# A projection slot between the value product and the next score pair, and lower halves 19 instead of 18 slots behind

## The chip, the cores and the metric

The kernel runs on one core of one Trainium2 chip. The metric is the device time of one execution in microseconds; the time of a kernel is the median of its runs.

## The reference

The kernel computes a gated mix of two branches over the same input `x` of 2048 tokens with 512 features, all in float32.

```python
def ref(x, wqkv, wo, w_gate, w_up, w_down, gate_w):
    g = sigmoid((x * gate_w).sum(-1, keepdims=True))
    # branch a: 32 heads of 16 features, each query sees the 256 keys up to itself
    q, k, v = split_heads(x @ wqkv)
    scores = where(mask, q @ k.T * 16 ** -0.5, -1e9)
    a = merge_heads(softmax(scores) @ v) @ wo
    # branch b: hidden width 1376
    b = (sigmoid(x @ w_gate) * (x @ w_up)) @ w_down
    return g * a + (1 - g) * b
```

## The kernel before

Products of float32 accuracy are made of three products of shorter operands: each operand is split into a high and a low part, and high times high, high times low and low times high are summed in PSUM. For the projections (queries and keys, called `pj`; gate and up, called `gu`) one output tile of 128 x 512 takes 12 such matmuls, 4 blocks of the contraction times 3.

The 32 heads are worked in 8 groups of 4, and the 2048 tokens in 16 blocks of 128. One step `u` of the main loop is one block of one group, so there are 128 steps and some more to drain. In a step the 4 heads `hh` are gone through one after the other. For each head one **turn** is put into TensorE's queue:

- `s_part` (line 296): scores with queries on partitions, into a PSUM tile `s`. VectorE takes the row maximum of it (line 302, tile `junk`, then `mx`).
- `st_part` (line 342): scores of block `u - 9` with keys on partitions, into a PSUM tile `st`, of another head. ScalarE takes the exponential of it into `pt` (line 347). The two score matmuls use 64 rows of the array each, one the upper and one the lower 64, so that they run side by side: a score pair.
- a stretch of **slots** of the projections. `turns()` is a generator. In slot number t it issues one matmul for the upper 64 rows of the contraction (matmul t of a long list in which each projection tile has 12), and one for the lower 64 rows, which stands `SHIFT` slots further back in the list. The two run side by side on the two halves of the array and both add into PSUM. So a projection tile (a **group**) occupies its PSUM buffer for 12 slots of its upper half and until `SHIFT` slots later its lower half is through too. A turn takes `GAP` = 3 slots; the fourth turn of an odd step takes none. Two steps so have 7 turns with 21 slots.

When the lower half of a group is through, `turns()` appends its evacuation to the list `evac`: ScalarE copies the PSUM tile to SBUF (`gu_post`, line 466, or `proj_raw`, line 240), and what follows from that copy (a DMA of it, the next weights' split by `gu_next`). `flush(evac)` is called after the score pair of each turn, so the copy stands in ScalarE's queue behind the exponential of that turn. The projections' PSUM pool `misc` has 3 buffers, so the first matmul of a group takes the buffer of the group three before it, and waits for that group's copy.

At the start of each even step, before the score pair of its first head, the **value products** `pv_part` of two earlier blocks are issued (line 378): matmuls with 32 columns of the array for each of 4 heads, which take all 128 rows.

Every 16th step and so on other work is spread in the same hand-made order: `split_wqk`, `split_gu` (the next weights' high and low parts), `max_split`, `o_take` (line 394, evacuation of `pv`), and DMAs on SyncE's queue, collected in `later` and issued at the head of a step. The order of the instructions on TensorE, ScalarE, VectorE and SyncE is the order written (the schedule is manual); the framework only adds the waits between engines.

After the main loop come the drain steps (`u` of 128 and more, no `s_part`), in which six slots stand after each second head, and then the down projection (`pd`) and the output projection (`pa`), which the change doesn't touch.

```python
for half, v in enumerate((t, t - SHIFT)):
    if 0 <= v < n_rest * k3:
        groups[v // k3][0](v % k3, half)
if t >= SHIFT and (t - SHIFT) % k3 == k3 - 1:
    _, after, post = groups[(t - SHIFT) // k3]
    evac.append(lambda after=after, post=post: (post(), after()))
```

Of the kernel before, what the change touches and what calls it, by code (L numbers as in the profile page):

```python
# [36 lines left out]
PVLAG = LAG + 2  # L37
# [1 line left out]
QB = 32  # L39
HOLD = 3  # L40
GAP = 3
SHIFT = 18
WD_LATE = {1: 8, 2: 9, 5: 10}
AHEAD = 5

# [2 lines left out]
def gated_mix_kernel(  # L48
# [48 lines left out]
    NU = NG * NB  # L97
# [15 lines left out]
    with ExitStack() as actx:  # L113
# [12 lines left out]
        def load_wqk(g):  # L126
            raw = cpool.tile([P, ND, P], F32, tag="wqraw", name=f"wqraw{g}", bufs=2)
            nc.sync.dma_start(raw, wqk[g])
            return raw
# [126 lines left out]
        def stack_build(t):  # L256
            sh, sl = (v.bitcast(F32) for v in stg.pop(t))
            rt = ring[t % RING].bitcast(F32)
            st = rt.rearrange("(a r) j f -> r a j f", r=4)
            dmas = [fill_rows(t % RING, 0, 0)]  # L260
            for low in range(2):
                for j in range(4):
                    for r in range(3):
                        if low == (r == (1 if j < 2 else 2)):
                            dmas.append((st[r + 1, :, j], (sl if low else sh)[32 * j:32 * j + 32]))
            return dmas
# [52 lines left out]
        def max_store(s):  # L319
            nt = nms.pop(s)  # L320
            dst = max_d[s].rearrange("h l b (a t) -> a (h l b) t", t=QB)
            for a in range(P // QB):
                nc.sync.dma_start(dst[a], nt[a * QB:(a + 1) * QB])
# [40 lines left out]
        evac = []  # L364
# [4 lines left out]
        def pv_part(u):  # L369
            g, j = divmod(u, NB)  # L370
            p = pts.pop(u)
            last = min(NB, j + 3)
            q = j
            while q < last:
                e = min(last, (q // 4 + 1) * 4)
                for hh in range(HG):
                    h = g * HG + hh
                    mm(  # L378
                        pv[32 * hh:32 * hh + 32, (q % 4) * P:(q % 4 + e - q) * P],
                        V[:, j, h * VW:h * VW + 32],  # L380
                        p[:, hh, (q - j) * P:(e - j) * P],
                        start=False, stop=True, skip_group_check=True,
                        tile_position=(0, 32 * hh),
                    )
                q = e
            if j % 2 == 1:
                extras.append(lambda: o_take(g * NC + j // 4, j // 2 % 2))

        def o_take(s, half):
            g, c = divmod(s, NC)  # L390
            if half == 0:
                obs[s] = cpool.tile([P, CH], F32, tag="ob", name=f"ob{s}", bufs=2)
            cols = slice(2 * P * half, 2 * P * half + 2 * P)
            nc.scalar.copy(obs[s][:, cols], pv[:, cols])
            nc.vector.memset(pv[:, cols], 0.0)
            if half == 0:
                return
            ob = obs.pop(s)
            for hh in range(HG):
                h = g * HG + hh  # L400
                later.append((oT_d[h * DH:(h + 1) * DH, c * CH:(c + 1) * CH], ob[32 * hh:32 * hh + DH]))
            later.append((sum_d[c, g * HG:(g + 1) * HG], ob.rearrange("(h r) f -> r h f", r=32)[DH]))
# [38 lines left out]
        def load_gu(f, w):  # L441
            raw_gu[f, w] = cpool.tile([P, D], F32, tag="draw", name=f"guraw{f}_{w}", bufs=2)
            src = wgu[f, w] if FCH[f] == P else wgu_tail[w, :, :, 0:width(f, w)]
            nc.sync.dma_start(gu_half(raw_gu[f, w], width(f, w)), src)
# [69 lines left out]
        def turns():  # L514
            k3 = 3 * ND
            groups = []
            for t in range(n_rest * k3 + SHIFT):
                if t and t % GAP == 0:
                    yield
                if t % k3 == 0 and len(groups) < n_rest:  # L520
                    groups.append((work or rest).pop(0))
                for half, v in enumerate((t, t - SHIFT)):
                    if 0 <= v < n_rest * k3:
                        groups[v // k3][0](v % k3, half)
                if t >= SHIFT and (t - SHIFT) % k3 == k3 - 1:
                    _, after, post = groups[(t - SHIFT) // k3]
                    evac.append(lambda after=after, post=post: (post(), after()))

        def flush(acts):
            while acts:  # L530
                acts.pop(0)()
# [24 lines left out]
        def flat(v, c):  # L556
            return v[c].rearrange("h (q t) -> (h q) t", t=P)
# [5 lines left out]
        def sums_invert(c):  # L563
            t = sm.pop(c)
            nc.vector.reciprocal(t, t)
            return flat(rec_d, c), t

        n_first = len(first) * 3 * ND + 2 * 3 * ND
        n_rest = len(rest) + NSTEP - 6 - HOLD
# [4 lines left out]
        WD = NU - 5  # L574
        done = 0
        slots = turns()
        sdma = []

        for u in range(N):
            if u == LAG:  # L580
                vctx.close()
                ppool = actx.enter_context(tc.tile_pool(name="ppool", bufs=1))
            if u == 4:
                load_gu(0, 0)
                load_gu(0, 1)
            if u % 8 == 1 and u > 8 and u // 8 + 1 < NP:
                sdma = stack_build(u // 8 + 1)
            if u % 16 == 8 and u // 16 + 2 < NG:
                raw_q = load_wqk(u // 16 + 2)
            if u % 4 == 0 and 0 < u <= NU:  # L590
                max_store(u // 4 - 1)
            run_dmas(later)
            later.clear()
            run_dmas(sdma[:SD])
            del sdma[:SD]
            if u % 4 == 1 and 1 < u <= NU + 1:
                max_load(u // 4 - 1)
            if WD <= u < WD + 16 and (u - WD) % 2 == 0:
                load_d((u - WD) // 2)
            s4 = {1: 4, 5: 5, 9: 6, U_LAST: NSTEP - 2, U_LAST + 1: NSTEP - 1}.get(u)  # L600
            if u % 4 == 3 and u > LAG and (u + 2) // 4 + 4 < NSTEP - 2:
                s4 = (u + 2) // 4 + 4
            if s4 is not None:
                if u < LAG:
                    (work if u == 1 else first).append((3 * ND, lambda k, s4=s4: proj_mm(s4, k), lambda s4=s4: proj_post(s4)))
                else:
                    work.append(proj_group(s4))
            for hh in range(HG):
                if hh == 0 and u % 2 == 0:
                    for w in (u - PVLAG - 1, u - PVLAG):  # L610
                        if 0 <= w < NU:
                            pv_part(w)
                if u < NU:
                    s_part(u, hh)
                if 0 <= u - LAG < NU:
                    st_part(u - LAG, hh ^ 1 if u < NU else hh)
                flush(evac)
                flush(behind)
                if u >= LAG and (hh < HG - 1 or u % 2 == 0 if u < NU else hh % 2 == 1):
                    next(slots, None)  # L620
                    if u >= NU:
                        next(slots, None)
            flush(extras)
            extras.extend(extras_next)
            extras_next.clear()
            if u < LAG - 1:
                done += run_first(n_first * (u + 1) // LAG - done)
            elif u < LAG:
                run_first(n_first - done - 3 * ND)
                split_gu(0, 0)  # L630
                split_gu(0, 1)
                flush(behind)
                run_first(3 * ND)
                done = 0
            if u % 4 == 3 and u < NU:
                max_split(u // 4)
            if u // 16 + 2 < NG:
                if u % 16 == 13:
                    split_wqk(u // 16 + 2, raw_q, 0)
                if u % 16 == 14:  # L640
                    split_wqk(u // 16 + 2, raw_q, 1)
            if 0 <= u - LAG < NU:
                mask_p(u - LAG)
            if WD + 2 <= u < WD + 10 and (u - WD) % 2 == 0:
                split_d((u - WD) // 2 - 1)
            if SUMS <= u and (u - SUMS) % 4 == 0:
                sums_load((u - SUMS) // 4)
            if SUMS + 2 <= u and (u - SUMS) % 4 == 2:
                later.append(sums_invert((u - SUMS) // 4))
            if u >= HLOAD and (u - HLOAD) % 2 == 0:  # L650
                h_load((u - HLOAD) // 2)
            if u >= N - 2:
                h_skew(u - N - 1)
# [162 lines left out]
```

## Time and profile before

| what | value |
|---|---|
| median of 3 runs | 772.11 us (771.64 to 774.44) |
| the profiled execution: time, span | 771.27 us, 769.6 us |
| TensorE (PE) busy | 754.3 us, 98% |
| VectorE (DVE) busy | 477.4 us, 62% |
| ScalarE (ACT) busy | 438.9 us, 57% |
| GpSimd (POOL) busy | 169.1 us, 22% |
| DMA | 103.57 MB, mean 135 GB/s |

PE stands for TensorE's matmuls and PEld for its weight loads. In a group's row of the profile stand its instructions' busy time, the mean duration of one in ns, and the time that the engine stood idle just before them with what ended it. Rows of the timeline begin with start and duration in us, and end with the idle time before in brackets.

### The profile page before, as it was taken

To read this page: it belongs to the slowest core of one execution; us is meant where nothing else is said; L and a number is where in the kernel's file an instruction comes from. 1 tells how busy PE (TensorE), PEld (TensorE's weight loads), DVE (VectorE), ACT (ScalarE), POOL (GpSimd) and SP (SyncE) were. 2 spreads that over 40 slices of the span, in tenths; PEclk is the share of its full clock that TensorE was granted. 3 is DMA by queue.
4 is the path that set the end of the run, shared out by engine and by line. 5 is a ranking of instruction groups with operands and counts; after the bars stand their busy time and mean duration, and the time that the engine had idled before them with its cause. 6 is when DMAs were issued, how large, how long until landed. Compare 5 with 4: busy or idle time off the path is not lost.

```text
span 769.6 us, 17398 instructions
## 1 busy us (share of the span) xinstructions
PE 754.3 (98%) x6180; PEld 575.0 (75%) x6180; DVE 477.4 (62%) x1459; ACT 438.9 (57%) x930; POOL 169.1 (22%) x256
## 2 busy tenths in 40 slices
PE   8999999999999999999999999999999999999998
PEld 6877777776867777777777777777775778888886
DVE  5356766666676666666666677567621694739371
ACT  5412666676666666666667666665765563625341
POOL 7000333232233232323323322332331000000000
PEclk9999999999999999999999999999999999999999
DMA  8340424425443353342543425443265786647351
GB/s 300 91 111 18 114 86 107 135 81 159 118 106 110 119 138 111 92 137 84 159 126 94 121 69 146 136 129 100 99 190 174 229 253 205 202 163 244 109 162 55
DMA packets 69958, 103.57 MB, mean 135 GB/s; under 512 B 19314, under 2 KB 29042, under 8 KB 69872
## 3 DMA queue, kind: packets, MB, share of 16 engines
q1 hardware_dynamic: 69872, 102.48, 45.3%
q8 instruction: 48, 0.79, 0.4%
q14 instruction: 38, 0.31, 0.1%
HBM read 45.26 MB, written 32.00 MB: 100 GB/s over the span
## 4 chain that ended last, share of the span: by engine, by line
PE 83%; DVE 5%; ACT 4%; DMA 3%; issue 2%; SPq 1%; POOLq 0%; ACTq 0%; DVEq 0%
PE gu L228 30%; PE pv L378 9%; PE pj L228 8%; PE s L296 8%; PE st L342 5%; PE pd L72 4%; PE pd L70 4%; PE pd L71 4%; PE vps L70 2%; PE vps L71 2%; PE vps L72 2%; PE pa L70 2%; PE pa L72 2%; PE pa L71 2%; DVE junk L302 1%
## 5 line engine op out<-in xcount | busy, mean ns | idle before, releaser
L347 ACT ACTIVATE pt<-st 128x384 f32<-128x384 f32 (+2 forms) x512 | 241.1, 474 | 182.8 <-PE st L342 79.1
L228 PE MATMUL gu<-xh,w 64*128 64x512 f32 (+2 forms) x1384 | 343.4, 392 | 0.0
L302 DVE CUSTOM_DVE_ANT_0 junk<-s,mask 128x384 f32<-128x384 f32 (+2 forms) x512 | 270.4, 528 | 114.7 <-PE st L342 42.3
L228 PE MATMUL gu<-xl,w 64*128 64x512 f32 (+2 forms) x692 | 226.3, 392 | 0.0
L228 PEld LDWEIGHTS gu<-xh,w 64*128 64x128 f32 (+3 forms) x1384 | 189.0, 183 | 20.6 <-issue 0.2
L296 PE MATMUL s<-ring 64*128 64x384 f32 (+2 forms) x536 | 169.8, 339 | 6.6 <-DVE mx L302 5.3
L342 PE MATMUL st<-ring 64*128 64x384 f32 (+2 forms) x536 | 173.1, 338 | 0.0
L352 POOL TENSOR_SCALAR_AFFINE_SELECT pt<-pt 128x512 f32<-128x512 f32 x128 | 82.3, 643 | 402.0 <-ACT pt L347 398.4
L296 PEld LDWEIGHTS s<-ring 64*128 64x128 f32 x536 | 94.2, 184 | 60.7 <-DVE mx L302 37.0
L228 PEld LDWEIGHTS gu<-xl,w 64*128 64x128 f32 (+2 forms) x692 | 107.0, 183 | 5.9
L342 PEld LDWEIGHTS st<-ring 64*128 64x128 f32 x536 | 96.1, 184 | 12.3 <-issue 1.4
L378 PE MATMUL pv<-pt,V 128*32 128x384 f32 (+2 forms) x1408 | 91.0, 388 | 1.7 <-POOL pt L352 1.7
L228 PE MATMUL pj<-xh,wqh 64*128 64x512 f32 (+1 forms) x232 | 91.0, 397 | 0.7 <-ACT xh L66 0.7
L228 PE MATMUL pj<-xl,wqh 64*128 64x512 f32 (+1 forms) x232 | 90.8, 396 | 0.4 <-DVE xl L67 0.4
L357 POOL TENSOR_SCALAR_AFFINE_SELECT pt<-pt 128x512 f32<-128x512 f32 x112 | 77.3, 690 | 0.0
L228 PE MATMUL pj<-xh,wql 64*128 64x512 f32 (+1 forms) x232 | 71.6, 395 | 0.0
L72 PE MATMUL pd<-ring,hb 128*128 128x512 f32 (+1 forms) x176 | 69.4, 394 | 0.3 <-DVE hb L67 0.3
L70 PE MATMUL pd<-ring,hb 128*128 128x512 f32 (+1 forms) x176 | 69.5, 395 | 0.0
L71 PE MATMUL pd<-ring,hb 128*128 128x512 f32 (+1 forms) x176 | 68.8, 391 | 0.4 <-DVE ring L67 0.4
L378 PEld LDWEIGHTS pv<-pt,V 128*32 128x32 f32 x1408 | 37.3, 109 | 36.9 <-issue 28.8
L66 ACT CAST hb<-V 128x512 fp32r<-128x512 f32 (+1 forms) x44 | 27.3, 621 | 54.5 <-DVE V L552 53.8
L466 ACT COPY sp<-gu 128x512 f32<-128x512 f32 (+2 forms) x88 | 51.0, 581 | 1.2 <-issue 1.2
(74 smaller groups left out, 900.0 us busy)
## 6 DMA issues: line engine op xcount, KB each, us to landing
gu_scratch<-sp SPq DMA_DIRECT2D x80, 256.0 KB
V<-gu_scratch SPq DMA_DIRECT2D x80, 256.0 KB
ring<-sh SPq DMA_DIRECT2D x128, 128.0 KB
ring<-sl SPq DMA_DIRECT2D x64, 128.0 KB
guraw<-in_wgu_dram SPq DMA_DIRECT2D x20, 256.0 KB
V<-in_xT_dram SPq DMA_DIRECT2D x16, 256.0 KB
oT_scratch<-ob SPq DMA_DIRECT2D x128, 32.0 KB
xl<-oT_scratch SPq DMA_DIRECT2D x16, 256.0 KB
```

The source lines that it names most:

```text
L70: mm(ps, lh, rh, start=first, stop=False)
L71: mm(ps, lh, rl, start=False, stop=False)
L72: mm(ps, ll, rh, start=False, stop=last)
L228: mm(pt[0:fw], (wl if w == 2 else wh)[r, d], (xl if w == 1 else xh)[r, d, c * CH:(c + 1) * CH], start=k == 0 and half != 1, stop=k == 3 * ...
L296: mm(pt[:, (k - k0) * P:(e - k0) * P], lhsT, blk(g, k, hh, 1, e - k), start=k == k0, stop=e == i + 1, skip_group_check=True,)
L302: nc.vector.tensor_tensor_reduce(junk[:, 0:n], pt[:, 0:n], mask[:, 3 * P - n:], scale=1.0, scalar=NEG, op0=ALU.add, op1=ALU.max, accum_out ...
L342: mm(pt[:, (q - j) * P:(e - j) * P], lhsT, blk(g, q, hh, 0, e - q), start=q == j, stop=e == last, skip_group_check=True,)
L347: nc.scalar.activation(pts[u][:, hh, 0:n], pt[:, 0:n], AF.Exp, scale=SCALE)
L352: nc.gpsimd.affine_select(p[:, :, 0:P], p[:, :, 0:P], pattern=[[0, HG], [1, P]], compare_op=ALU.is_ge, fill=0.0, base=0, channel_multiplie ...
L357: nc.gpsimd.affine_select(p[:, :, 2 * P:], p[:, :, 2 * P:], pattern=[[0, HG], [-1, P]], compare_op=ALU.is_gt, fill=0.0, base=0, channel_mu ...
L378: mm(pv[32 * hh:32 * hh + 32, (q % 4) * P:(q % 4 + e - q) * P], V[:, j, h * VW:h * VW + 32], p[:, hh, (q - j) * P:(e - j) * P], start=Fals ...
L466: nc.scalar.copy(t[0:width(f, w)], gp.pop((f, c, w))[0:width(f, w)])
```

## The change

`SHIFT` is 19 instead of 18. `turns()` yields after each slot instead of after each third, and `run_slots(n)` runs n of them. At the head of each even step, after the value products and before the score pair of its first head, `evac` is flushed and one slot is run. The first turn of that step then runs two slots instead of three, so that two steps have 21 slots as before (in the drain steps the turn after the second head gives the slot). Number and kinds of all instructions are the same as before on every engine.

```diff
-SHIFT = 18
+SHIFT = 19
...
             for t in range(n_rest * k3 + SHIFT):
-                if t and t % GAP == 0:
-                    yield
                 if t % k3 == 0 and len(groups) < n_rest:
...
                     evac.append(lambda after=after, post=post: (post(), after()))
+                yield
...
+        def run_slots(n):
+            for _ in range(n):
+                next(slots, None)
...
                         if 0 <= w < NU:
                             pv_part(w)
+                head = u > PVLAG and hh == 0 and u % 2 == 0
+                if head:
+                    flush(evac)
+                    run_slots(1)
                 if u < NU:
                     s_part(u, hh)
...
                 if u >= LAG and (hh < HG - 1 or u % 2 == 0 if u < NU else hh % 2 == 1):
-                    next(slots, None)
-                    if u >= NU:
-                        next(slots, None)
+                    run_slots((GAP if u < NU else 2 * GAP) - (u > PVLAG and u % 2 == 0 and hh == (0 if u < NU else 1)))
```

## The prediction, made before the changed kernel ran

> **What bounds the kernel now.** I read the page first: the span, the busy shares, the granted clock and the chain that ended last, then the costliest groups.
>
> ```profile
> span 769.6 us, 17398 instructions
> ...
> PE 754.3 (98%) x6180; PEld 575.0 (75%) x6180; DVE 477.4 (62%) x1459; ACT 438.9 (57%) x930; POOL 169.1 (22%) x256
> ...
> PEclk9999999999999999999999999999999999999999
> ...
> PE 83%; DVE 5%; ACT 4%; DMA 3%; issue 2%; SPq 1%; POOLq 0%; ACTq 0%; DVEq 0%
> ...
> L228 PE MATMUL gu<-xh,w 64*128 64x512 f32 (+2 forms) x1384 | 343.4, 392 | 0.0
> L296 PE MATMUL s<-ring 64*128 64x384 f32 (+2 forms) x536 | 169.8, 339 | 6.6 <-DVE mx L302 5.3
> ```
>
> TensorE is the bound: 98% busy at full clock, 83% of the chain. It stands idle 15.3 us in the whole span, and the only idle time of weight inside the attention loop is before the score matmuls (6.6 us, mostly for VectorE's row maximum). Before the projection matmuls it is 0.0: no slot waits today. Since TensorE executes in order and has no slack, whatever makes one matmul wait is added to the time in full, and whatever takes idle time away can bring no more than these few us. The next view, the waits of TensorE alone, says the same:
>
> ```profile
> PE s L296 <- DVE mx L302: 5.3, 12, 0.8
> PE pv L378 <- POOL pt L352: 1.7, 1, 1.7
> ```
>
> There is no row in which a projection matmul in the loop waits for ScalarE, although every group takes a PSUM buffer that ScalarE must have copied out. How near that copy comes to being late is read in the timeline of one turn, here one in which a group (pj) has just ended:
>
> ```profile
> 306.83 0.33 PE L342 MATMUL st<-ring 64*128 64x384 f32 x1
> 306.84 0.34 PE L296 MATMUL s<-ring 64*128 64x384 f32 x1
> 307.00 0.40 PE L228 MATMUL gu<-xh,w 64*128 64x512 f32 x2
> 307.24 0.40 PE L228 MATMUL gu<-xl,w 64*128 64x512 f32 x2
> 307.24 0.49 ACT L347 ACTIVATE pt<-st 128x384 f32<-128x384 f32 x1 [0.39 <-PE s L296]
> 307.47 0.40 PE L228 MATMUL gu<-xh,w 64*128 64x512 f32 x2
> 307.63 0.58 ACT L240 COPY pr<-pj 128x512 f32<-128x512 f32 x1
> 307.70 0.33 PE L296 MATMUL s<-ring 64*128 64x384 f32 x1
> 307.71 0.33 PE L342 MATMUL st<-ring 64*128 64x384 f32 x1
> 307.87 0.39 PE L228 MATMUL gu<-xh,w 64*128 64x512 f32 x1
> 308.57 0.34 PE L342 MATMUL st<-ring 64*128 64x384 f32 x1
> 308.74 0.39 PE L228 MATMUL pj<-xh,wqh 64*128 64x512 f32 x1
> ```
>
> A turn is 0.87 us: the score pair 0.17 (306.83 to 307.00), then three slots of 0.23. The group's last matmul was the slot before 306.83. The exponential of this turn begins at 307.24, the copy behind it at 307.63, and the copy ends at 308.21 (307.63 + 0.58). The third group after it takes the freed buffer at 308.74, two turns after the pair at 306.83. So the copy is 0.53 us ahead of its user, which is less than one turn.
>
> **The change, part by part.**
>
> *The lag of 19.* A group begins at slot 12n and ends at slot 12n + 29 before, 12n + 30 after; its buffer is wanted at slot 12n + 36 in both. Turns end at slots divisible by 3. So before, the last matmul closes a turn, and the copy is queued with the next turn's exponential. After, the last matmul opens a turn (or is the head slot); two more slots follow it, and the copy is queued only behind the exponential of the turn after that. In ScalarE's order the copy therefore stands one exponential, one turn of 0.87 us, further back, while its user stays where it was. In the rows above it is as if the user came at 307.87, with the copy still ending at 308.21: 0.34 us late.
>
> What a late release costs beyond its lateness is read where VectorE releases a score matmul late:
>
> ```profile
> 216.64 0.49 ACT L347 ACTIVATE pt<-st 128x384 f32<-128x384 f32 x1 [0.26 <-PE s L296]
> 217.87 0.08 DVE L302 DVE_READ_ACCUMULATOR2_ANT mx<- 128x1 f32 x1
> 218.00 0.18 PEld L296 LDWEIGHTS s<-ring 64*128 64x128 f32 x1 [1.17 <-DVE mx L302]
> 218.01 0.45 PE L296 MATMUL s<-ring 64*128 64x384 f32 x1 [0.74 <-DVE mx L302]
> 218.01 0.18 PEld L342 LDWEIGHTS st<-ring 64*128 64x128 f32 x1
> 218.29 0.39 PE L228 MATMUL gu<-xh,w 64*128 64x512 f32 x2
> ```
>
> VectorE is done at 217.95 (217.87 + 0.08) and the weight load starts at 218.00: 0.05 us. It is the weight load that waits, so it is not hidden behind an earlier matmul: from the score pair to the next slot it is 0.28 us here, against 0.17 in the turn above, 0.11 more. One late group thus costs 0.34 + 0.05 + 0.11 = 0.50 us. Behind the waiting load stand, in TensorE's one queue, the lower half of the same slot, the other slots of the turn and the next score pair, and so the next row maximum and the next exponential: nothing on TensorE gets past it.
>
> *How many groups are late.* 21 slots make two steps, and 12 slots a group, so the pattern repeats every 7 groups (84 slots, 4 pairs of steps). Counting from the head slot, the last matmuls fall on slots 0, 3, 6, 9, 12, 15 and 18 of the 21, once each. For 3, 6, 9 and 12 the copy's exponential and the user are separated by three slots and one score pair, as above: late. For 15 and 18 the value products stand in between, and these take far longer than what is missing:
>
> ```profile
> 302.68 1.51 PE L378 MATMUL pv<-pt,V 128*32 128x256 f32 x32
> 304.11 0.18 PEld L296 LDWEIGHTS s<-ring 64*128 64x128 f32 x1 [0.41 <-issue]
> 304.12 0.44 PE L296 MATMUL s<-ring 64*128 64x384 f32 x1
> 304.40 0.38 PE L228 MATMUL gu<-xh,w 64*128 64x512 f32 x1
> ```
>
> 1.44 us (302.68 to 304.12) against 0.39 us. For 0, the head slot itself, the copy follows the exponential of the first head, five slots and two pairs ahead of its user: 0.17 + 5 x 0.23 + 2 x 0.17 = 1.66 us from that st matmul, against 1.38 (306.83 to 308.21) + 0.05 for the copy; no wait. So 4 groups of 7. In the order of the changed kernel's instructions I count 58 such groups in the loop (of some 101) with exactly three slots and one pair between; 58 x 0.50 = 29.0 us.
>
> *The drain.* There six slots stand together after two score matmuls. Three late groups have only the second of those st matmuls between the exponential and the user, so the user is due 0.17 us after the st that the copy's exponential reads: 1.38 - 0.17 + 0.05 + 0.11 = 1.37 us each, 4.1 us together.
>
> *The head slot.* After the value products a weight load is exposed today: from s at 304.12 to the first slot at 304.40 it is again 0.28 instead of 0.17. With the slot in between, the slot's own load is the exposed one, and the score pair's load hides behind the slot. That is the same 0.11 us in another place, so I put it at nothing. What the slot can give is time to VectorE, whose late maxima cost 6.6 us. At the row above the load's idle time is not VectorE's ("issue"), so little of that lies at the value products. But each new wait of 0.50 us also gives VectorE time to catch up. Between none and all of the 6.6 us I take half, 3.3 us off, as the late maxima come at other places of the 21 slots than the new waits about as often as not.
>
> *What else moves.* Each copy's DMA is collected for the head of the next step, so a copy one turn later may send its store one step later; the queue is SyncE's and the stored tiles are read again only in the last phase, behind many slots. ScalarE (57% busy) has the same copies:
>
> ```profile
> L466 ACT COPY sp<-gu 128x512 f32<-128x512 f32 (+2 forms) x88 | 51.0, 581 | 1.2 <-issue 1.2
> L240 ACT COPY pr<-pj 128x512 f32<-128x512 f32 x26 | 15.1, 581 | 0.0
> ```
>
> All have 581 ns, so the turn shown stands for both kinds. The value products wait for the mask of the last exponential once, 1.7 us; the drain's order changes, so that this wait may vanish or come twice: 0, plus or minus 1.7.
>
> **Sum.** 771.27 us for the profiled execution (span 769.6), + 29.0 + 4.1 - 3.3 = 801.1 us. The median of the runs is 0.84 us over that execution (772.11), so 801.9, say 802 us.
>
> **A rule of the skill against a row.** The Trainium skill ("TensorE: Matmul & The Clock Gate", Part 2, step-by-step) says that the queue pulls weight loads ahead of matmuls in flight when row groups don't conflict. By that the lower half's load at least would go ahead while the upper half's waits, and if the waiting one were ready too, the reload would be no cost: 61 x 0.11 = 6.7 us less. The row speaks against it: at 218.01 the load of st, in the other half of the rows and with its buffer read out since 217.13 (216.64 + 0.49), starts only with that of s.
>
> **The rivals.**
>
> *No reload at a late group* (chance 0.14). The wait is there, but the weights load in its shade: 61 x 0.11 = 6.7 us less, 795.2 us. For it: weight loads usually run one slot ahead (TensorE's loads are 75% busy and hidden). Against it: the 0.28 at 218.01. The rule just named would give this time.
>
> *The head slot is what counts, and the kernel is faster* (0.05). If the copies were in time, the slot after the value products would cover VectorE's late maxima (6.6 us) and, if its load were ready early, the 0.11 at each of about 64 value products (7.0 us): 772.1 - 13.6 = 758.5 us. It decides for this side if the copy is done by about 307.64 in the rows above, one slot before its user, so 0.57 us earlier than the row has it; nothing in the change makes the exponential or the copy start sooner in the four late places.
>
> *Nothing measurable* (0.03). The waits are absorbed, because TensorE's idle time for VectorE falls by as much as the new waits bring. That needs 33 us of idle time to take from, and there are 6.6.
>
> *More than the sum* (0.04). A late group also delays the next exponential and maximum, and these in turn the value products or a score pair: one more 0.50 us for half of the 58 groups, 14.5 us more, 816 us. Against it: while TensorE waits, ScalarE and VectorE only catch up.
>
> **How the numbers follow.** The forecast, 802 us, has 0.74. Its bounds: all 6.6 us of VectorE's waits gone and no reload, 772.1 + 33.1 - 6.6 - 6.7 = 791.9; nothing absorbed and the mask's wait twice, 772.1 + 33.1 + 1.7 = 806.9. With about 1.5 us on either side for the median (the runs shown spread over 2.8 us), the range is 790 to 808, which holds the rival without reload too. What can be told from no change is about 0.5%, 3.9 us. Faster by more: 0.05; within: 0.03; slower: 0.74 + 0.14 + 0.04 = 0.92.
>
> **What would show it.** In the profile after, the groups of L228 should have idle time before them that ScalarE's copies of sp and pr (L466, L240) ended, in about 60 waits, where today there is none. The profile shows the score pair before as busy until 308.04 (307.71 + 0.33) and the late user would start at 308.26 (308.21 + 0.05), so about 0.2 us of each wait shows as idle time of the matmuls, some 13 us, and the rest as longer spacing; the value products should be followed by a slot and not a pair, with 0.11 us more to the next start as now. The idle time before s (L296) should be below 6.6 us. The forecast is wrong if the projection matmuls still show no idle time, or if the copies follow the first exponential after a group's end.

## The result, and the profile after

The changed kernel takes 797.22 us (median, 795.51 to 797.97), the kernel before 772.37 us with the runs taken beside it. The ratio is 1.031, with a 95% interval of 1.0297 to 1.0328. The forecast was 802 us, in a range of 790 to 808.

The profiled execution takes 795.51 us with a span of 793.8 us, 24.2 us more than the one before in both. The page of it, to be laid beside the page before: the busy shares, the clock, the chain, and the costliest groups of TensorE.

```profile
span 793.8 us, 17420 instructions
...
PE 765.3 (96%) x6180; PEld 571.7 (72%) x6180; DVE 483.9 (61%) x1459; ACT 438.6 (55%) x930; POOL 174.3 (22%) x256
...
PEclk9999999999999999999999999999999999999999
...
PE 76%; ACT 9%; DVE 6%; DMA 4%; issue 2%; SPq 2%; POOL 0%; ACTq 0%; POOLq 0%; DVEq 0%
...
L228 PE MATMUL gu<-xh,w 64*128 64x512 f32 (+3 forms) x1384 | 362.0, 399 | 9.4 <-ACT sp L466 6.7
...
L296 PE MATMUL s<-ring 64*128 64x384 f32 (+2 forms) x536 | 161.8, 325 | 6.5 <-DVE mx L302 6.4
```

ScalarE has risen from 4% to 9% of the chain though it is no busier (438.6 us against 438.9). The projection matmuls, which waited for nothing, now stand idle 9.4 us in this group alone, most of it until a copy of ScalarE ends. The granted clock was 0.998 before and 1.0 after. The waits of TensorE's matmuls say the same with counts:

```profile
PE gu L228 <- ACT sp L466: 6.7, 20, 1.0
PE s L296 <- DVE mx L302: 6.4, 20, 0.7
PE pj L228 <- ACT pr L240: 3.3, 11, 0.6
PE gu L228 <- ACT pr L240: 2.7, 12, 0.2
...
PE pv L378 <- POOL pt L352: 1.0, 1, 1.0
```

43 waits for the two kinds of copies with 12.7 us of idle time, in place of none. One of them in the timeline, where the copy of a pj tile is followed by its user:

```profile
300.11 0.49 ACT L347 ACTIVATE pt<-st 128x384 f32<-128x384 f32 x1 [0.38 <-PE st L342]
...
300.50 0.58 ACT L240 COPY pr<-pj 128x512 f32<-128x512 f32 x1
...
300.58 0.33 PE L296 MATMUL s<-ring 64*128 64x384 f32 x1
...
301.13 0.18 PEld L228 LDWEIGHTS gu<-xh,w 64*128 64x128 f32 x1 [0.59 <-ACT pr L240]
301.13 0.50 PE L228 MATMUL gu<-xh,w 64*128 64x512 f32 x1 [0.22 <-ACT pr L240]
301.13 0.29 PEld L228 LDWEIGHTS gu<-xl,w 64*128 64x128 f32 x2
...
301.47 0.62 PE L228 MATMUL gu<-xh,w 64*128 64x512 f32 x2
```

The copy ends at 301.08 and the weight load starts at 301.13, 0.05 us later. Without the wait the slot would have followed the pair by 0.17, at 300.75: it is 0.38 us late, and the next slot follows after 0.34 (301.13 to 301.47) instead of 0.23. That is 0.49 us for one late group, of which the profile shows only 0.22 as idle time of the matmuls, because the pair's modelled end covers the rest.

### The profile page after: what moved, and what is told of

It is laid out like the page before. It is cut to its first block, busy times and chain, and to the rows that moved or that the text cites. A ratio compares the mean times of both kernels' runs of the same rounds, so it can differ in the third digit from the quotient of the medians.

```text
span 793.8 us, 17420 instructions
## 1 busy us (share of the span) xinstructions
PE 765.3 (96%) x6180; PEld 571.7 (72%) x6180; DVE 483.9 (61%) x1459; ACT 438.6 (55%) x930; POOL 174.3 (22%) x256
## 4 chain that ended last, share of the span: by engine, by line
PE 76%; ACT 9%; DVE 6%; DMA 4%; issue 2%; SPq 2%; POOL 0%; ACTq 0%; POOLq 0%; DVEq 0%
PE gu L228 26%; PE pv L378 9%; PE pj L228 8%; PE s L296 5%; PE pd L72 4%; PE pd L70 4%; PE pd L71 4%; PE st L342 4%; ACT pt L347 3%; PE vps L70 2%; ACT sp L466 2%; DVE sl L254 2%; PE vps L71 2%; PE vps L72 2%; PE pa L70 2%
## 5 line engine op out<-in xcount | busy, mean ns | idle before, releaser
L228 PE MATMUL gu<-xh,w 64*128 64x512 f32 (+3 forms) x1384 | 362.0, 399 | 9.4 <-ACT sp L466 6.7
L228 PE MATMUL gu<-xl,w 64*128 64x512 f32 (+3 forms) x692 | 250.6, 403 | 0.0
L228 PEld LDWEIGHTS gu<-xh,w 64*128 64x128 f32 (+3 forms) x1384 | 203.6, 183 | 53.1 <-ACT sp L466 15.3
L352 POOL TENSOR_SCALAR_AFFINE_SELECT pt<-pt 128x512 f32<-128x512 f32 x128 | 81.5, 637 | 419.5 <-ACT pt L347 416.0
L296 PE MATMUL s<-ring 64*128 64x384 f32 (+2 forms) x536 | 161.8, 325 | 6.5 <-DVE mx L302 6.4
L342 PE MATMUL st<-ring 64*128 64x384 f32 (+2 forms) x536 | 164.3, 322 | 0.0
L228 PEld LDWEIGHTS gu<-xl,w 64*128 64x128 f32 (+3 forms) x692 | 122.8, 183 | 12.8 <-issue 6.4
L228 PE MATMUL pj<-xh,wqh 64*128 64x512 f32 (+1 forms) x232 | 96.5, 419 | 5.5 <-ACT pr L240 3.3
L357 POOL TENSOR_SCALAR_AFFINE_SELECT pt<-pt 128x512 f32<-128x512 f32 x112 | 83.3, 744 | 0.0
L228 PE MATMUL pj<-xh,wql 64*128 64x512 f32 (+1 forms) x232 | 74.7, 400 | 0.0
L228 PEld LDWEIGHTS pj<-xh,wqh 64*128 64x128 f32 (+1 forms) x232 | 43.3, 187 | 27.0 <-issue 7.5
```

Of the source, the lines that this page charges most:

```text
L228: mm(pt[0:fw], (wl if w == 2 else wh)[r, d], (xl if w == 1 else xh)[r, d, c * CH:(c + 1) * CH], start=k == 0 and half != 1, stop=k == 3 * ...
L296: mm(pt[:, (k - k0) * P:(e - k0) * P], lhsT, blk(g, k, hh, 1, e - k), start=k == k0, stop=e == i + 1, skip_group_check=True,)
L342: mm(pt[:, (q - j) * P:(e - j) * P], lhsT, blk(g, q, hh, 0, e - q), start=q == j, stop=e == last, skip_group_check=True,)
L352: nc.gpsimd.affine_select(p[:, :, 0:P], p[:, :, 0:P], pattern=[[0, HG], [1, P]], compare_op=ALU.is_ge, fill=0.0, base=0, channel_multiplie ...
L357: nc.gpsimd.affine_select(p[:, :, 2 * P:], p[:, :, 2 * P:], pattern=[[0, HG], [-1, P]], compare_op=ALU.is_gt, fill=0.0, base=0, channel_mu ...
```

## The experiments

### The two parts apart

The head slot alone, with the lag at 18:

```diff
-SHIFT = 19
+SHIFT = 18
```

> The head slot stays, the lag goes back to 18 slots. Lag theory (the loss is the copy queued one exponential later): every group again has 12 slot matmuls and two score pairs between the copy's exponential and its user, so no projection matmul waits for ScalarE, and the time is that of the kernel before less what the slot gives to late row maxima: 772 us, between 766 and 774. Slot theory (the loss is the slot after the value products, through its exposed weight load or a later score pair): 790 to 797 us, with the projection matmuls still without waits.

Measured: 772.78 us, ratio to the kernel before 1.0003 (0.9987 to 1.0018). The waits of TensorE for VectorE and GpSimd in its loop are those of the kernel before, to the digit, and no projection matmul in the loop waits for a copy:

```profile
PE s L296 <- DVE mx L302: 5.3, 12, 0.8
PE pv L378 <- POOL pt L352: 1.7, 1, 1.7
```

The slot costs nothing and gives nothing that can be told in the time. Where its exposed weight load went is seen in the waits of the weight loads ("issue": no wait that the profile shows). Before:

```profile
PEld s L296 <- DVE mx L302: 37.0, 76, 1.3
...
PEld s L296 <- issue: 14.2, 33, 0.6
```

With the slot:

```profile
PEld s L296 <- DVE mx L302: 23.5, 49, 1.3
PEld gu L228 <- issue: 15.4, 41, 0.6
PEld pj L228 <- issue: 8.2, 14, 0.6
...
PEld s L296 <- issue: 2.9, 8, 0.4
```

The loads of s that came first after the value products have become loads of gu and pj in the same place.

The lag alone, in the kernel before:

```diff
-SHIFT = 18
+SHIFT = 19
```

> The kernel before with a lag of 19 slots and no head slot. Lag theory: in the order of its instructions 73 groups of the loop (5 of 7) have only three slots and one pair between, and 6 of the drain have one st alone; if 40 of 58 are really late as in the changed kernel, 73 x 40/58 x 0.49 + 6 x 1.2 = 32 us more than before, 804 us, and above the changed kernel. Slot theory: 772 to 778 us.

Measured: 805.32 us, ratio 1.0401 (1.0374 to 1.0428). The lag gives all of the loss, and more of it than in the changed kernel: without the head slot 5 groups of 7 end where they are late, instead of 4. By its timeline 64 of the 73 groups of the loop wait, and all 6 of the drain. That the time is so near the expected 804 us is partly chance: the expectation had about 50 of the 73 late. By their spacing the late groups cost some 38 us, of which 32.7 show in the time.

```profile
PE gu L228 <- ACT sp L466: 13.2, 36, 1.1
PE s L296 <- DVE mx L302: 4.7, 16, 0.7
PE pj L228 <- ACT pr L240: 3.4, 11, 0.6
PE gu L228 <- ACT pr L240: 2.9, 13, 0.2
```

So the slot, as such worth nothing, saves 8 us once the lag is 19. It moves one of the 7 places, so that the order has 58 late places in the loop and 3 in the drain instead of 73 and 6.

### Is it the place of the copy in ScalarE's queue?

A group that ends one slot later could be late by itself. To take the queue's order apart from that, the evacuations are flushed ahead of each score pair; TensorE's order stays that of the changed kernel.

```diff
+                flush(evac)
                 if u < NU:
                     s_part(u, hh)
```

> The changed kernel (slot and lag of 19) with the list of evacuations flushed ahead of each score pair instead of behind it, so that the copy stands before that turn's exponential in ScalarE's queue; TensorE's order is unchanged. Lag theory: the copy starts about 0.85 us earlier, the waits of projection matmuls for ScalarE vanish, 772 us, between 766 and 775. If the lateness comes from the group's later end itself or from the slot, it stays at 795 to 797.

Measured: 766.53 us, ratio 0.9908 (0.9888 to 0.9928). The loss is gone, with the slot and the lag of 19 in place, so it is the copy's place behind one exponential too many. That it is 6 us faster than the kernel before is the lower end of what was expected (772 us, between 766 and 775). Of TensorE's matmuls in the loop these still wait:

```profile
PE s L296 <- DVE mx L302: 2.9, 11, 0.3
...
PE pv L378 <- POOL pt L352: 1.0, 1, 1.0
```

No group of the loop waits for its copy any more. Three of the drain do, but only at their weight loads, with 1.1 us of idle time there.

### Why more groups should have been late than were

In the changed kernel 47 of the 58 groups that I had counted are late by its timeline; of the 43 waits above 40 lie in the loop and 3 in the drain. The other 11 all look like this one (timeline after):

```profile
293.56 0.77 DVE L254 TENSOR_TENSOR sl<-pr,sh 128x512 fp32r<-128x512 f32 x1 [0.50 <-ACT sh L250]
...
294.38 0.27 DVE L395 MEMSET pv<- 128x256 f32 x1
...
294.66 0.58 ACT L466 COPY sp<-gu 128x512 f32<-128x512 f32 x1
295.03 0.08 DVE L302 DVE_READ_ACCUMULATOR2_ANT mx<- 128x1 f32 x1
295.16 0.18 PEld L296 LDWEIGHTS s<-ring 64*128 64x128 f32 x1 [0.70 <-DVE mx L302]
295.16 0.45 PE L296 MATMUL s<-ring 64*128 64x384 f32 x1 [0.26 <-DVE mx L302]
...
295.45 0.40 PE L228 MATMUL gu<-xh,w 64*128 64x512 f32 x1
```

The subtraction for a projection's low part (L254) and the clearing of pv have held up the row maximum, TensorE already waits for that at the score pair, and by the time the slot comes the copy (ended 295.24) is done. To see whether such a wait stands in the shade of the other, the subtraction goes to GpSimd:

```diff
-            nc.vector.tensor_tensor(sl, pj.pop(s), sh.bitcast(F32), op=ALU.subtract)
+            eng.tensor_tensor(sl, pj.pop(s), sh.bitcast(F32), op=ALU.subtract)
...
-            extras.append(lambda: extras_next.append(lambda: (proj_hi(s), proj_lo(s))))
+            extras.append(lambda: extras_next.append(lambda: (proj_hi(s), proj_lo(s, nc.gpsimd))))
```

> The changed kernel with the subtraction that makes the low part of a projection (line 254, 0.77 to 0.87 us) on GpSimd instead of VectorE; the orders of TensorE and ScalarE are unchanged. Shade theory: about 14 groups of the 58 show no wait for ScalarE because a row maximum made late by that subtraction already held TensorE at the score pair before; with the maximum in time they wait for ScalarE instead. Waits of the projection matmuls for sp and pr rise from 43 to some 55, those of s for mx fall from 20 to under 8, and the time moves by less than 3 us. Rival: the late maxima come on top of the late groups, then the time falls by the 3.5 to 5 us that they cost and the 43 stay.

Measured: 796.2 us, ratio to before 1.0291 (1.0268 to 1.0314), which is not told apart from the changed kernel. Its matmuls' waits for s fell from 20 to 7; those for copies stayed at 43 as far as they show as idle time. The weight loads tell it better, changed kernel first:

```profile
PEld s L296 <- DVE mx L302: 17.5, 28, 1.1
PEld gu L228 <- ACT sp L466: 15.3, 23, 1.4
```

and with the subtraction on GpSimd:

```profile
PEld gu L228 <- ACT sp L466: 19.6, 35, 1.4
...
PEld s L296 <- DVE mx L302: 14.5, 30, 1.4
```

12 loads more wait for the copy of sp, and by the timeline all 58 groups are late. The wait changed its owner and the time stayed: the shade theory holds. The expected 55 waits at matmuls were a miss in where to look: a wait short enough to lie under the pair's modelled end shows at the load and not at the matmul.

### Where the gain of the copy-first order comes from

> The kernel before (no slot, lag of 18) with the evacuations flushed ahead of each score pair. The run with slot, lag of 19 and the copy first came out at 766.5 us, below the kernel before. Cast theory: that gain is the copy-first order alone, since with the copy the next weights' cast (line 452) also goes ahead of the exponential, and VectorE no longer stands waiting for it (18.1 us in 20 waits before) while row maxima queue behind: 765 to 768 us here too, waits of s for mx about 3 us instead of 6.6. Slot-and-lag theory: the slot or the lag gave it, and this kernel stays at 770 to 774 us.

Measured: 769.07 us, ratio 0.9951 (0.9933 to 0.997): half of the gain, between what the two theories expected. The waits of s for mx are 4.4 us, not the expected 3.

> Slot after the value products, lag of 18, copy first. Cast theory: 765 to 768 us, the same as without slot and as with the lag of 19. If the lag of 19 is worth something once the copy is early (two slots lie between a group's last matmul and the copy, so that ScalarE doesn't wait for it at the head of its queue), this kernel is 1 to 4 us above the one with 19.

Measured: 769.6 us, ratio 0.9956 (0.994 to 0.9971), which is 3.1 us above the kernel with the lag of 19.

> Lag of 19 and copy first, without the slot after the value products. Cast theory and lag theory: 765 to 768 us, since the slot only moves the exposed weight load from the score pair to itself. If the slot gives VectorE time, this is 1 to 4 us slower than 766.5.

Measured: 765.36 us, ratio 0.9909 (0.9888 to 0.993).

| copy first | no slot | head slot |
|---|---|---|
| lag 18 | 769.07 us | 769.6 us |
| lag 19 | 765.36 us | 766.53 us |

The slot again makes no difference. The lag of 19, which lost 24 to 33 us with the old order, is 3 to 4 us better than 18 with the new one. VectorE's own waits point to a reason: its subtraction for the next weights (L453) stood waiting for ScalarE's cast of them, with row maxima queued behind, and these waits fall with the time. Before, with lag 18 and copy first, and with lag 19 and copy first (no slot):

```profile
DVE w L453 <- ACT w L452: 18.1, 20, 2.7
```

```profile
DVE w L453 <- ACT w L452: 8.3, 17, 2.3
```

```profile
DVE w L453 <- ACT w L452: 1.6, 7, 0.3
```

With lag 18 and copy first the copy stands at the head of ScalarE's queue while the group's last matmul is just being issued; with 19 two slots have passed by then. That this is what brings cast and subtraction on in time is argued, not shown by itself.

If late maxima are what is left, taking the subtraction L254 off VectorE should now show in the time. The same edit as above, with slot, lag 19 and copy first:

> Slot, lag of 19, copy first, and the low-part subtraction of the projections on GpSimd. With no late groups left, late maxima are the only waits of TensorE in the loop (2.9 us of idle time and some 0.1 us of reload at each of 11): if the subtraction makes them, 763 to 766 us and waits of s for mx below 1.5 us; if other work of VectorE makes them, 766 to 767 us.

Measured: 762.0 us, ratio 0.9866 (0.9844 to 0.9888), 1 us below the range of the first branch. No wait of s for mx is left among TensorE's matmuls, as that branch had it. Two more, to see which parts this needs:

> Copy first, lag of 19, the low-part subtraction on GpSimd, and no slot after the value products. If the slot is worth nothing: 762 us, the same within 2 us as the kernel with it. If the slot gives VectorE time where its maxima are nearly late: 1 to 3 us slower, with waits of s for mx.

> The same with the lag of 18, so the kernel before with only the copy first and the subtraction on GpSimd. If the 3.7 us between the lags of 18 and 19 (copy first) came from late row maxima, it is within 1 us of the lag of 19 and above it only by waits of s for mx that remain; if it came from ScalarE waiting for the group's last matmul at the head of its queue, it stays 2 to 4 us slower.

Measured: 761.62 us, ratio 0.9853 (0.9832 to 0.9873), and 762.53 us, ratio 0.9864 (0.984 to 0.9888). Neither the slot nor the lag makes a difference that can be told any more, so ScalarE's wait for the group's last matmul is not what separated the lags. What separated them came through late row maxima: 0.4 us in 2 waits are left of them with the lag of 18 and none with 19. VectorE still waits for the cast with the lag of 18, almost as long as with L254 on VectorE (8.3 us above):

```profile
DVE w L453 <- ACT w L452: 7.3, 14, 2.3
```

So that wait costs TensorE little by itself. It cost time where VectorE had the subtraction L254 to do as well. The fastest version, with lag 19, copy first, no slot and the subtraction on GpSimd, has these waits of TensorE in its loop:

```profile
PE pv L378 <- POOL pt L352: 1.0, 1, 1.0
...
PE gu L228 <- ACT sp L466: 0.2, 1, 0.2
```

It is 1.5% faster than the kernel before. Two edits do it, the earlier flush and the engine of one subtraction; what the lag of 19 adds to them lies within the noise (0.9853 against 0.9864). The subtraction on GpSimd alone, in the kernel before, was not run.

## Why the prediction was right, point by point

- **The copy is one exponential further back, its user is not.** Shown: the lag alone loses (1.0401), the copy first with the same lag does not (0.9908). The places are right too: none of the 44 other groups of the loop is late.
- **One late group costs 0.34 + 0.05 + 0.11 = 0.50 us.** 0.49 in the timeline; over the 47 late groups of the loop, what their pair-to-slot and slot-to-slot spacing is over 0.17 and 0.23 us sums to 22.4 us, 0.48 each. With the 58 all late (subtraction on GpSimd) it is 27.9 us, against 29.0 in the sum.
- **58 late groups.** This is the term of the sum that was mis-sized. The order of instructions gives the places, but 11 of the 58 were held by a late row maximum one pair earlier: 22.4 us instead of 29.0. The forecast of some 13 us of idle time at about 60 matmuls came out at 12.7 us partly by luck: there are 43 such waits, and the drain's three are long, close to 1 us each.
- **The drain, 4.1 us.** Three waits. In the first the st matmul that the copy's exponential reads starts at 578.32, so the user was due at 578.49, and it started at 579.78.

```profile
578.32 0.48 PE L342 MATMUL st<-ring 64*128 64x384 f32 x2
...
578.76 0.49 ACT L347 ACTIVATE pt<-st 128x384 f32<-128x384 f32 x1 [0.50 <-POOL pt L352]
579.15 0.58 ACT L466 COPY sp<-gu 128x512 f32<-128x512 f32 x1
...
579.78 0.49 PE L228 MATMUL gu<-xh,w 64*128 64x512 f32 x1 [0.98 <-ACT sp L466]
...
580.12 0.62 PE L228 MATMUL gu<-xh,w 64*128 64x512 f32 x2
```

  1.29 us late and 0.11 for the reload (0.34 to the next slot) make 1.40 against 1.37, and the three together 4.1 us. The exponential starts 0.44 us behind its st here, where the prediction had 0.41, and by its row it waited for GpSimd's mask; the prediction had no such wait.
- **The head slot at nothing.** Shown by 1.0003, and by the loads that changed names. After the value products the changed kernel's pair follows the head slot by 0.34 us where slots else take 0.23 (297.85 and 298.19 in its timeline): the same 0.11, in another place.
- **3.3 us off for late maxima.** The sign I could not show in the way I named: the idle time before s was to fall below 6.6 us and stayed at 6.5 (20 waits instead of 12 with releaser mx). Of the 26.5 us of late groups and drain, the stretch from the first slot to the last value products shows only 22.8 us more, so about 3.7 us were given back. 0.7 of them are the last value products' own wait for GpSimd's mask, 1.0 us instead of 1.7. The weight loads of s that wait for mx fell from 76 to 28, 27 of these 48 by the slot (76 to 49 with the slot alone) and 21 by the lag. That these 21 shorter waits are the other 3 us is argued, not shown. Another 1.3 us of the 24.2 arose before the first slot, where both kernels have the same instructions. It is no part of the change: the slot alone and the copy first begin their slots 0.9 and 1.1 us earlier than the kernel before.
- **The rule against the row.** By the Trainium skill ("TensorE: Matmul & The Clock Gate", Part 2, step-by-step) weight loads are pulled ahead of matmuls in flight where row groups don't conflict. That did not spare the reload here. In the late group at 301.13 the load for the other half of the rows, which belongs to a group in mid-course and had nothing of its own to wait for, starts only with the one that waits, and the next slot is 0.11 us later than usual. In turns without a wait a load starts a slot ahead of its matmul (300.12 for the matmul at 300.34, just before this group); here the load that waited held back the one behind it. The rival without reload (795.2 us) came nearer to the time than the forecast, 2.0 us off against 4.8, but by the wrong way: the reload is there, and fewer groups pay it.
- **The other rivals.** The slot does not make the kernel faster; the new waits were not absorbed, since VectorE's waits had far less to give; and late groups did not cost more than their sum, since the time came out below it.

## What to carry to other kernels

Before a lag or a slot is moved in a hand-made order, work out for each PSUM buffer which instruction of the evacuating engine its copy stands behind and how many turns lie between that and the buffer's next user: the margin here was 0.53 us, and one place further back in the queue was 0.87. The cure was the copy's place in the queue, not the lag: with the evacuations flushed ahead of the exponential the same lag lost nothing. And count waits at the weight loads too, since a wait shorter than the last matmul's modelled end costs time without showing as idle time.

## What the runs showed that I had not expected

- The slot after the value products moves the exposed weight load by name and changes no time that can be told in any of four pairs (772.78 to 772.63 us, 769.6 to 769.07, 766.53 to 765.36, 762.0 to 761.62; the third pair's ratios to before are 0.9908 and 0.9909).
- The subtraction takes longer on GpSimd than on VectorE, and with the copy first the kernel is still faster with it there (762.0 against 766.53 us), as row maxima no longer queue behind it. In the changed kernel, with its late groups, it brought no change that can be told. The instructions on tile sl (min, median and max in ns), first in the fastest version, then in the kernel before:

```profile
L254 POOL TENSOR_TENSOR sl<-pr,sh x26: 1281/1298/1307, 94.4 to 456.3; 128x512 fp32r<-128x512 f32 x26
```

```profile
L254 DVE TENSOR_TENSOR sl<-pr,sh x26: 679/770/1034, 91.3 to 465.3; 128x512 fp32r<-128x512 f32 x26
```

  1298 ns at the median on GpSimd, 770 on VectorE.
